# First expert's weights loaded and split during attention, with a guessed expert

## The chip, the cores and the metric

The kernel runs on one core of a Trainium2 chip. The metric is the device time of one execution in microseconds (us). Matmuls run on TensorE (PE; PEld is its weight load), elementwise work on VectorE (DVE), ScalarE (ACT) and GpSimd (POOL); SyncE (SP) issues most of the transfers.

## The reference

Three layers follow one another on 2304 tokens (4 batches of 576) of width 512:

```python
scores = scale * np.matmul(q, k.transpose(0, 1, 3, 2))      # 8 heads of 64
scores = np.where(masks[None], scores, -1e9)                 # 4 heads: window 32; 4 heads: window 128, every 4th
attn = softmax(scores);  x = (attn @ v), heads side by side  # (2304, 512)

logits = x @ w_gate + modality_bias[modality_id]             # 8 experts, 2 modalities
e_idx = argmax(logits);  gate_w = softmax(logits)[e_idx]
out[mask_e] = gate_w * (relu(x[mask_e] @ w1[e]) @ w2[e])     # 512 -> 1024 -> 512, one expert per token

h = relu(x @ w_in);  out = (h * h) @ w_out                   # 512 -> 2048 -> 512
```

`modality_bias` is drawn with a spread of 0.5, and it decides most of the routing. In the inputs used here both modalities have their largest bias at expert 1 (0.93 and 0.47). After two batches expert 1 has 989 tokens and expert 4 has 163; after all four they have 1982 and 322, and no other expert has any.

## The kernel before

**Precision.** Matrices of the two later layers are split into a high part (`Copy` on ACT into the reduced type) and a low part (source minus high part, on DVE); each product is three matmuls: high by high, high by low, low by high.

**Attention** works in 48 units of 96 queries by 4 heads. `schedule` runs one round per unit and writes the order of all engines out by hand. In round i, PE gets the mask and the scores of unit i (`A`, lines 335 and 338), the transposes of the attention output x of unit i-5 (`H`, L413), the transposes of the probabilities of unit i-2 (`D`, L360) and their product with v for unit i-3 (`F`, L374). DVE gets the row maximum `nm` of unit i (L341), the low part `xtl` of unit i-5 (L417), and for unit i-3 the sum, reciprocal and scaled output `rs`, `rc`, `x` (L377, L380, L383). ACT gets the high part `xth` (L416), the copy `pt` of the transposes (L362) and last the exponentials `p` of unit i (L350, four instructions). Before the experts start, `H` has one PSUM bank, so its transposes wait until `xtl` of the round before has read it. Every sixth round and the next have the logits' matmuls (L434). Six units share a load of q, k and v on SP; POOL scales q (L316). Each unit's x goes to DRAM (`xd`) by SP.

**Routing.** After every batch of 12 units, `batch` routes it in small steps between the attention's instructions: about 30 DVE instructions of 0.15 to 0.3 us, one-hots, a table of token numbers. From the second batch on, `select` names the slots that are full: an expert and 128 of its tokens. It writes for each slot the expert, whether it differs from the slot before (`esel`), and where the tokens stand.

**Experts.** A slot j is gathered from `xd` by an indirect DMA (`begin`), transposed and split (`tx`, L747 to L749), multiplied with w1 (`l1`, 24 matmuls of 512 columns, L761), transposed again (`th`) and multiplied with w2 (`l2`, 24 more, L791). There are 25 slots in the program; 19 are run here, and their weights change only where the expert does. Slots come in waves: 2 after the second batch, 4 after the third, the rest after the fourth. `filler` puts slot work into the attention's rounds, FILL units of cost (about 1 us each) per round.

**The first slot** is special: its expert is known only after the second batch is routed, so then SP loads w1 and w2 (2 MB each, L710), ACT and DVE split them; POOL takes the low part of the first two of the four pieces of w1 (L720), and the eight pieces of w2 are split between the steps of `l1`. Later slots load under a condition on SP (L708) and split under a branch (`split`, L727): they do both only when the expert changes.

**The last layer** (`Ffn`) starts when attention's memory is free; its w_in and w_out are decoded from 8-byte floats beside the slots and it takes the second half of the time (L1010, 384 columns, and L1064, 512 columns).

The functions that the change touches, with the line numbers of the profile:

Of the kernel before, what the change touches and what calls it, by code (L numbers as in the profile page):

```python
# [11 lines left out]
F32 = mybir.dt.float32  # L12
# [29 lines left out]
RATE, RATE1, RATE2, FILL, BURST, GAP = 0.35, 0.5, 0.5, 3.0, 0.0, 3  # L42
# [22 lines left out]
def body(ctx, tc, ins, out):  # L65
# [14 lines left out]
    g.nsl = const.tile([1, 1], I32, name="nsl")  # L80

# [31 lines left out]
def schedule(g, att, moe):  # L113
# [3 lines left out]
    early = None  # L117
    i = 0
# [37 lines left out]
    for i in itertools.count():  # L156
        att.tail = i >= nu + 2
        ns, no, nh = (2, (5,), (5,)) if att.tail else (2, (5,), (6,)) if moe.ready else (3, (5, 4), (7,))
        r = RATE2 if i >= nu + 5 else RATE1 if moe.prepped else RATE
        if i == nu + 6:  # L160
            att.units.close()
            early = Early(g)
        if i == nu + 2:
            moe.banks((2, 4), (6, 0), (1, 1), (7, 3))
        att.A(i, (0, 1, 2)[:ns])
        if i == SETUP:
            att.setup()
        if NTL < i <= nu + 5 and i % NTL == 5:
            att.logits(i // NTL - 1, 1)
            if moe.ready and not att.tail:  # L170
                no, nh = nh, no
        if i > hold:
            step(r)
        att.H(i - 5, nh)
        filler(FILL / 2, False)
        att.D(i - 2)
        step(r)
        att.F(i - 3, no, one)
        att.C(i)
        filler(FILL / 2, True)  # L180
        step(r)
        if NTL < i <= nu + 5 and i % NTL == 4:
            att.logits(i // NTL - 1, 0)
        if due and side is None:
            moe.ready = sum(WAVES[due - 1])
            moe.pump()
            due = 0
        if nxt < B and side is None and i >= (nxt + 1) * UPB + 5:
            side = att.batch(nxt)
            due, sc, hold = nxt, 0.0, i + 1  # L190
            nxt += 1
        if not more:
            break
# [7 lines left out]
class Attention:  # L201
    def __init__(self, g, ctx):
# [27 lines left out]
        self.pref = al.tile([QT, E], F32, name="pref")  # L230
        self.tok = al.tile([QT, TPB], F32, name="tok")
# [24 lines left out]
    def setup(self):  # L256
# [20 lines left out]
        nc.vector.tensor_tensor(out=self.bias, in0=self.bias, in1=btmp, op=ALU.add)  # L277

    def bank(self):
        return self.g.bk[5 if self.tail else 6]  # L280
# [292 lines left out]
    def select(self, j0, n):  # L573
# [36 lines left out]
        if j0 == 0:  # L610
            yield 0.12
            nc.vector.memset(ef[:, 0:1], -1.0)
# [59 lines left out]
class Moe:  # L672
    def __init__(self, g, ctx):
# [10 lines left out]
        self.gx = [wp.tile([128, XW], F32, name=f"gx{i}") for i in range(3)]  # L684
        self.xh = wp.tile([128, 4, 128], F32R, name="xh")
        self.xl = wp.tile([128, 4, 128], F32R, name="xl")
        self.y = [wp.tile([128, XW], F32, name=f"y{i}") for i in range(2)]
# [14 lines left out]
    def stage(self, j, w):  # L702
# [4 lines left out]
        if j:  # L707
            nc.sync.dma_start(out=self.st[w], in_=src, cond=c, cond_hint=False)  # L708
        else:
            nc.sync.dma_start(out=self.st[w], in_=src)  # L710

    def split(self, j, w):
# [5 lines left out]
        def part(k, eng=nc.vector):  # L718
            nc.scalar.activation(out=hi[:, k, :], in_=src[:, k, :], func=AF.Copy)
            eng.tensor_tensor(out=lo[:, k, :], in0=src[:, k, :], in1=hi[:, k, :].bitcast(F32), op=ALU.subtract)  # L720

        if j == 0:
            for k in range(n):
                part(k, nc.gpsimd if w == 0 and k < 2 else nc.vector)
                yield -1
            return
        with tc.If(c > 0, preferred_fallthrough_block=False):  # L727
            for k in range(n):
                part(k)
# [83 lines left out]
    def prep(self, j):  # L813
# [4 lines left out]
        yield from self.split(j, 0)  # L818
# [6 lines left out]
    def main(self, j):  # L825
# [3 lines left out]
        w2 = self.split(0, 1) if j == 0 else iter(())  # L829
        for c in self.l1(j):  # L830
            next(w2, None)
            yield c
# [7 lines left out]
        yield from self.split(j, 1) if j else w2  # L840
# [319 lines left out]
```

## Time and profile before

| | |
|---|---|
| median of 3 runs | 801.3 us (796.3, 801.3 and 968.0) |
| the profiled execution | 797.15 us, of which the span of the trace is 795.4 us |
| mean granted TensorE clock | 0.997 |
| PE busy | 773.7 us, 97% of the span |
| PE weight load | 668.5 us, 84% |
| DVE busy | 413.0 us, 52% |
| ACT busy | 325.2 us, 41% |
| POOL busy | 170.0 us, 21% |

The times that follow are from the profiled execution and count from the start of its span. PE is busy nearly throughout, so the shares say little; what counts is where PE is not busy, and how many microseconds that is. Attention alone runs from 6 to about 117 us, attention with the first slots to about 160 us, the other slots to about 390 us, and the last layer to the end.

### The profile page before, as it was taken

How to read it: one execution, taken by the hardware profiler on the slowest of the kernel's cores; microseconds unless marked ns; L12 is line 12 of the kernel's file. 1: busy time of each engine (PE TensorE's matmuls, PEld its weight loads, DVE VectorE, ACT ScalarE, POOL GpSimd, SP SyncE). 2: the span in 40 equal slices, each digit the busy share in tenths (PEclk: the TensorE clock that was granted, in tenths of full speed). 3: DMA queues.
4: the chain of work that ended last, by engine and by line, in shares of the span. 5: the costliest groups of instructions: out<-in, count | busy, mean ns of one | idle time of the engine just before them, and what ended most of it. 6: DMA issues, size and time to landing. Idle time of an engine off the chain costs nothing.

```text
span 795.4 us, 12643 instructions
## 1 busy us (share of the span) xinstructions
PE 773.7 (97%) x4273; PEld 668.5 (84%) x4273; DVE 413.0 (52%) x1136; ACT 325.2 (41%) x779; POOL 170.0 (21%) x222
## 2 busy tenths in 40 slices
PE   8999997999999999999999999999999999999996
PEld 5888875778888888887888999999998998999985
DVE  5787889568456777452389822332242233234232
ACT  5877767334345545552245422222232232232221
POOL 4145632226323333201034400010010001001001
PEclk9999999999999999999999999999999999999999
DMA  8666773235534444451445210010010001001001
GB/s 228 178 165 176 179 250 100 74 93 148 172 111 128 134 112 129 146 185 55 147 147 160 67 40 27 14 41 27 1 54 0 27 14 40 1 0 40 1 1 40
DMA packets 49130, 72.65 MB, mean 91 GB/s; under 512 B 7296, under 2 KB 31712, under 8 KB 48544
## 3 DMA queue, kind: packets, MB, share of 16 engines
q1 hardware_dynamic: 43040, 56.00, 24.3%
q0 software_dynamic: 3280, 10.76, 4.4%
q10 hardware_dynamic: 2736, 4.99, 1.7%
q8 instruction: 35, 0.57, 0.3%
q14 instruction: 39, 0.32, 0.1%
HBM read 132.27 MB, written 17.06 MB: 188 GB/s over the span
## 4 chain that ended last, share of the span: by engine, by line
issue 40%; PE 9%; POOL 2%; POOLq 0%; DVE 0%
PE bk L1010 4%; PE bk L1064 4%; POOL out L1069 2%; PE bk L791 1%; PE bk L993 0%; POOLq L1156 0%; DVE fout L1068 0%; POOLq L1069 0%
## 5 line engine op out<-in xcount | busy, mean ns | idle before, releaser
L1020 DVE TENSOR_TENSOR fsq<-fr 128x384 f32<-128x384 f32 x96 | 53.4, 557 | 163.6 <-ACT fr L1018 163.5
L1010 PE MATMUL bk<-yh,wih 128*128 128x384 f32 x384 | 130.0, 338 | 2.1 <-ACTq L860 1.4
L1010 PE MATMUL bk<-yh,wil 128*128 128x384 f32 x384 | 129.2, 336 | 0.0
L1010 PE MATMUL bk<-yl,wih 128*128 128x384 f32 x384 | 129.0, 336 | 0.0
L1018 ACT ACTIVATE fr<-bk 128x384 f32<-128x384 f32 x96 | 47.0, 490 | 193.0 <-PE bk L1010 192.4
L1064 PE MATMUL bk<-woh,fhh 128*128 128x512 f32 x288 | 113.2, 393 | 0.0
L1064 PE MATMUL bk<-woh,fhl 128*128 128x512 f32 x288 | 112.7, 391 | 0.0
L1064 PE MATMUL bk<-wol,fhh 128*128 128x512 f32 x288 | 112.6, 391 | 0.0
L1069 POOL DMA_INDIRECT out<-fout,fidx x18 | 17.6, 978 | 322.1 <-DVE fout L1068 321.8
L1029 DVE TENSOR_TENSOR fhl<-fsq,fhh 128x384 fp32r<-128x384 f32 x96 | 55.3, 576 | 44.3 <-ACT fhh L1028 44.1
L1010 PEld LDWEIGHTS bk<-yh,wih 128*128 128x128 f32 x384 | 72.2, 188 | 4.7 <-ACTq L860 1.7
L1010 PEld LDWEIGHTS bk<-yl,wih 128*128 128x128 f32 x384 | 72.2, 188 | 1.8
L1010 PEld LDWEIGHTS bk<-yh,wil 128*128 128x128 f32 x384 | 72.2, 188 | 0.0
L1028 ACT ACTIVATE fhh<-fsq 128x384 fp32r<-128x384 f32 x96 | 50.4, 525 | 51.1 <-DVE fsq L1020 50.9
L1064 PEld LDWEIGHTS bk<-woh,fhl 128*128 128x128 f32 x288 | 54.0, 188 | 12.3
L761 PE MATMUL bk<-w1h,xh 128*128 128x512 f32 x152 | 63.1, 415 | 0.8 <-DVE htl L777 0.8
L1064 PEld LDWEIGHTS bk<-wol,fhh 128*128 128x128 f32 x288 | 54.1, 188 | 9.6
L1064 PEld LDWEIGHTS bk<-woh,fhh 128*128 128x128 f32 x288 | 54.1, 188 | 9.5
L791 PE MATMUL bk<-w2h,hth 128*128 128x512 f32 x152 | 61.1, 402 | 0.0
L761 PE MATMUL bk<-w1h,xl 128*128 128x512 f32 x152 | 61.0, 401 | 0.0
L761 PE MATMUL bk<-w1l,xh 128*128 128x512 f32 x152 | 60.8, 400 | 0.0
L791 PE MATMUL bk<-w2h,htl 128*128 128x512 f32 x152 | 59.5, 391 | 0.0
(174 smaller groups left out, 1356.3 us busy)
## 6 DMA issues: line engine op xcount, KB each, us to landing
st<-in_w SPq DMA_DIRECT2D x41, 2048.0 KB
raw<-in_wi SPq DMA_DIRECT2D x32, 256.0 KB
raw<-in_wo SPq DMA_DIRECT2D x32, 256.0 KB
v<-in_v SPq DMA_DIRECT2D x7, 780.0 KB
q<-in_q SPq DMA_DIRECT2D x7, 576.0 KB
kd<-in_k SPq DMA_DIRECT2D x14, 288.0 KB
xd<-x SPq DMA_DIRECT2D x40, 96.0 KB
yb<-y ACTq DMA_DIRECT2D x13, 256.5 KB
```

The lines of the kernel that those rows point to most:

```text
L761: nc.tensor.matmul(ps, a[:, c, :], w[:, c, sl], start=k == 0, stop=k == 11)
L791: nc.tensor.matmul(ps, a[:, c, :], w[:, c, :], start=k == 0, stop=k == 23)
L1010: nc.tensor.matmul(ps, w[:, c, f * 128:(f + 1) * 128], a[:, c, :], start=k == 0, stop=k == 11)
L1018: nc.scalar.activation(out=r, in_=ps, func=AF.Relu)
L1020: nc.vector.tensor_tensor(out=s, in0=r, in1=r, op=ALU.mult)
L1028: nc.scalar.activation(out=hh, in_=s, func=AF.Copy)
L1029: nc.vector.tensor_tensor(out=hl, in0=s, in1=hh.bitcast(F32), op=ALU.subtract)
L1064: nc.tensor.matmul(acc[t], a[:, sl], w[:, f, :], start=f == 0 and j == 0, stop=f == NF - 1 and j == 2)
L1069: dma = nc.gpsimd.indirect_dma_start(out=out, out_offset=bass.IndirectOffsetOnAxis(ap=self.idx[:, i:i + 1].bitcast(U32), axis=0), in_=o, i ...
```

## The change

A guess of the first slot's expert is computed in `setup` from the modality bias alone: for each modality the experts with the largest bias are marked, and the guess is the marked expert of the lowest number (eight small DVE instructions, stored in a new 4-byte tile `guess`). A new generator `Moe.first` loads that expert's w1 and w2 in 16 pieces of 256 KB on SP and splits each piece two calls later, the high part on ACT and the low part on DVE. `schedule` calls it at the end of rounds: three rounds of four up to round 17, then even rounds in which no routing is under way or routing holds. What is left is run before the first wave is made ready. `select` starts with the guess in place of -1, so that the first slot loads and splits only if the guess was wrong, under the same condition and branch as later slots. In the first wave `filler` gets 2.0 units per round (FILL1) in place of 3.0. The routing's matmuls use bank 7 in place of 6 once slots are ready. `xh` and `xl`, the split inputs of `l1`, are allocated ahead of the gather buffers `gx`.

```diff
-RATE, RATE1, RATE2, FILL, BURST, GAP = 0.35, 0.5, 0.5, 3.0, 0.0, 3
+RATE, RATE1, RATE2, FILL, FILL1, BURST, GAP = 0.35, 0.5, 0.5, 3.0, 2.0, 0.0, 3
...
     g.nsl = const.tile([1, 1], I32, name="nsl")
+    g.guess = const.tile([1, 1], I32, name="guess")
...
+    first = moe.first()
...
-        filler(FILL / 2, False)
+        f = (FILL1 if moe.ready == WAVES[0][1] else FILL) / 2
+        filler(f, False)
...
-        filler(FILL / 2, True)
+        filler(f, True)
...
+        if i > SETUP and (i % 4 < 3 if i < UPB + 6 else i % 2 == 0 and (side is None or i < hold)):
+            next(first, None)
         if due and side is None:
+            run(first)
             moe.ready = sum(WAVES[due - 1])
...
+        self.first = al.tile([1, 16], F32, name="gfirst")[:, :1]
...
+        top = ac.tile([1, 2, 1], F32, name="gtop")
+        at = ac.tile([1, 2, E], F32, name="gat")
+        cum = ac.tile([1, E], F32, name="gcum")
+        nc.vector.tensor_reduce(out=top, in_=mb[0:1], axis=AX.X, op=ALU.max)
+        nc.vector.tensor_tensor(out=at, in0=mb[0:1], in1=top.to_broadcast([1, 2, E]), op=ALU.is_equal)
+        nc.vector.tensor_tensor(out=at[:, 0], in0=at[:, 0], in1=at[:, 1], op=ALU.max)
+        nc.vector.tensor_tensor_scan(out=cum, data0=at[:, 0], data1=at[:, 0], initial=0.0, op0=ALU.add, op1=ALU.bypass)
+        nc.vector.tensor_scalar(out=at[:, 1], in0=cum, scalar1=0.5, scalar2=None, op0=ALU.is_lt)
+        nc.vector.tensor_reduce(out=self.first, in_=at[:, 1], axis=AX.X, op=ALU.add)
+        nc.vector.tensor_scalar(out=self.first, in0=self.first, scalar1=float(E - 1), scalar2=None, op0=ALU.min)
+        nc.vector.tensor_copy(g.guess, self.first)
 
     def bank(self):
-        return self.g.bk[5 if self.tail else 6]
+        return self.g.bk[5 if self.tail else 7 if self.g.moe.ready else 6]
...
-            nc.vector.memset(ef[:, 0:1], -1.0)
+            nc.vector.tensor_copy(ef[:, 0:1], self.first)
...
-        self.gx = [wp.tile([128, XW], F32, name=f"gx{i}") for i in range(3)]
         self.xh = wp.tile([128, 4, 128], F32R, name="xh")
         self.xl = wp.tile([128, 4, 128], F32R, name="xl")
+        self.gx = [wp.tile([128, XW], F32, name=f"gx{i}") for i in range(3)]
...
-        if j:
-            nc.sync.dma_start(out=self.st[w], in_=src, cond=c, cond_hint=False)
-        else:
-            nc.sync.dma_start(out=self.st[w], in_=src)
+        nc.sync.dma_start(out=self.st[w], in_=src, cond=c, cond_hint=False)
+
+    def first(self):
+        nc, ins = self.g.nc, self.g.ins
+        e = nc.values_load(self.g.guess[0:1, 0:1], engines=(ET.SP,), min_val=0, max_val=E - 1)
+        parts = []
+        for w in range(2):
+            st, hi, lo = (x[w].rearrange("p c f -> p (c f)") for x in (self.st, self.wh, self.wl))
+            src = ins["w1" if w == 0 else "w2"][bass.ds(e, 1)].rearrange("o p c f -> p (o c) f")
+            for k in range(8):
+                parts.append([x[:, k * 512:(k + 1) * 512] for x in (st, src, hi, lo)])
+        for i in range(len(parts) + 2):
+            if i < len(parts):
+                nc.sync.dma_start(out=parts[i][0], in_=parts[i][1])
+            if i > 1:
+                st, _, hi, lo = parts[i - 2]
+                nc.scalar.activation(out=hi, in_=st, func=AF.Copy)
+                nc.vector.tensor_tensor(out=lo, in0=st, in1=hi.bitcast(F32), op=ALU.subtract)
+            yield
...
-        def part(k, eng=nc.vector):
-            nc.scalar.activation(out=hi[:, k, :], in_=src[:, k, :], func=AF.Copy)
-            eng.tensor_tensor(out=lo[:, k, :], in0=src[:, k, :], in1=hi[:, k, :].bitcast(F32), op=ALU.subtract)
-
-        if j == 0:
-            for k in range(n):
-                part(k, nc.gpsimd if w == 0 and k < 2 else nc.vector)
-                yield -1
-            return
         with tc.If(c > 0, preferred_fallthrough_block=False):
             for k in range(n):
-                part(k)
+                nc.scalar.activation(out=hi[:, k, :], in_=src[:, k, :], func=AF.Copy)
+                nc.vector.tensor_tensor(out=lo[:, k, :], in0=src[:, k, :], in1=hi[:, k, :].bitcast(F32), op=ALU.subtract)
...
-        yield from self.split(j, 0)
+        self.split(j, 0)
...
-        w2 = self.split(0, 1) if j == 0 else iter(())
-        for c in self.l1(j):
-            next(w2, None)
-            yield c
+        yield from self.l1(j)
...
-        yield from self.split(j, 1) if j else w2
+        self.split(j, 1)
```

In the built program the 16 splits stand at the end of rounds 6; 8, 9, 10; 12, 13, 14; 16, 17, 18; 22; 24; 26; 28; 30 and 34. Line numbers shift by 7 to 25; L742 is the new low part, L741 the new high part, L738 the new load.

The first place is DVE in rounds 7 to 9 of the attention (x closes a round, nm opens the next; xtl is the low part for the logits). Before:

```order
L383 TENSOR_TENSOR x<-bk_72,rc 96x256
L341 TENSOR_REDUCE nm<-bk_68 96x4
L417 TENSOR_TENSOR xtl<-bk_75,xth 128x2x96
L377 TENSOR_SCALAR rs<-bk_73 96x4
L380 RECIPROCAL rc<-rs 96x4
L383 TENSOR_TENSOR x<-bk_73,rc 96x256
L341 TENSOR_REDUCE nm<-bk_69 96x4
```

and with the change:

```order
L401 TENSOR_TENSOR x<-bk_72,rc 96x256
L742 TENSOR_TENSOR w1l<-st_84,w1h 128x512
L359 TENSOR_REDUCE nm<-bk_68 96x4
L435 TENSOR_TENSOR xtl<-bk_75,xth 128x2x96
L395 TENSOR_SCALAR rs<-bk_73 96x4
L398 RECIPROCAL rc<-rs 96x4
L401 TENSOR_TENSOR x<-bk_73,rc 96x256
L742 TENSOR_TENSOR w1l<-st_84,w1h 128x512
L359 TENSOR_REDUCE nm<-bk_69 96x4
```

The low part stands between x and the next round's nm, so nm waits for it.

The second place is ACT in the same rounds, with the change (before, the rows are the same without L741):

```order
L368 ACTIVATE p<-bk_70,nm 96x128 x4
L741 ACTIVATE w1h<-st_84 128x512
L434 ACTIVATE xth<-bk_75 128x2x96
L380 ACTIVATE pt<-bk_71 128x384
L368 ACTIVATE p<-bk_68,nm 96x128 x4
L741 ACTIVATE w1h<-st_84 128x512
L434 ACTIVATE xth<-bk_75 128x2x96
```

The high part stands behind the exponentials of its round and ahead of the next round's xth; the low part on DVE needs it.

The third place is PE where the first slot begins (gx are its gathered tokens, w1h, w1l and xh, xl the operands of `l1`). Before, two attention rounds lie between the slot's transposes (gx) and its first matmuls; these are the last rows of the second:

```order
L374 MATMUL bk_73<-v,pt 96x65 x4
L335 LDWEIGHTS mask
L335 MATMUL bk_69<-mask 96x512
L338 MATMUL bk_69<-kd_145,q 96x256 x2
L413 MATMUL bk_74<-ident,x 128x96 x2
L360 MATMUL bk_71<-ident,p 128x96 x4
L374 MATMUL bk_73<-v,pt 96x65 x4
L761 MATMUL bk_70<-w1h,xh 128x512
L761 MATMUL bk_70<-w1l,xh 128x512
L761 MATMUL bk_70<-w1h,xl 128x512
```

With the change:

```order
L772 MATMUL bk_70<-ident,gx_95 128x128 x4
L378 MATMUL bk_71<-ident,p 128x96 x4
L392 MATMUL bk_73<-v,pt 96x65 x4
L751 UNCONDITIONAL_BRANCH
L786 MATMUL bk_70<-w1h,xh 128x512
L786 MATMUL bk_70<-w1l,xh 128x512
L786 MATMUL bk_70<-w1h,xl 128x512
```

The first matmuls follow the transposes in the same round, two rounds earlier.

## Rows read from the trace of the kernel before

**Rows 1.** Stages: length, busy time of each engine (instructions), PE clock, DMA share, GB/s.
```profile
20.00:100.00 80.00, 80.00 (x684) 68.08 (x682) 62.89 (x219) 61.22 (x203) 36.90 (x54) 1.00 0.69 175
100.00:120.00 20.00, 18.11 (x147) 14.58 (x147) 17.07 (x81) 12.93 (x43) 6.51 (x10) 1.00 0.76 257
120.00:140.00 20.00, 14.92 (x87) 11.29 (x85) 18.57 (x46) 14.49 (x34) 4.67 (x2) 0.91 0.30 87
140.00:160.00 20.00, 17.84 (x113) 14.03 (x112) 10.70 (x52) 5.96 (x13) 4.66 (x8) 1.00 0.27 71
400.00:780.00 380.00, 380.00 (x1950) 345.04 (x1949) 154.15 (x309) 113.00 (x240) 39.48 (x37) 1.00 0.11 35
```

**Rows 2.** PE's waits, 100 to 160 us: releaser, total us, times, longest.
```profile
PE bk L374 <- DVE x L383: 4.3, 3, 3.0
...
PE bk L434 <- DVE xtl L417: 0.8, 1, 0.8
...
PE bk L477 <- DVE xtl L417: 0.5, 1, 0.5
PE bk L434 <- DVE lt L438: 0.5, 1, 0.5
PE bk L451 <- DVE xtl L417: 0.5, 1, 0.5
```

**Rows 3.** Timeline at the first slot's split: start, duration, engine, instruction [idle before].
```profile
121.01 4.67 POOL L720 TENSOR_TENSOR w1l<-st,w1h 128x1024 fp32r<-128x1024 f32 x2 [10.36 <-ACT w1h L719]
...
121.50 1.89 DVE L526 CAST rrf<-rri 96x6 f32<-96x6 int32 x1
...
127.46 0.89 PE L374 MATMUL bk<-v,pt 128*96 128x65 f32 x8 [3.05 <-DVE x L383]
```

**Rows 4.** Timeline, the first slot's first matmuls on PE, first and last of seven.
```profile
128.85 0.63 PE L761 MATMUL bk<-w1h,xl 128*128 128x512 f32 x1
...
131.41 0.63 PE L761 MATMUL bk<-w1h,xl 128*128 128x512 f32 x1
```

**Rows 5.** Timeline of one plain attention round, 35.04 to 37.28 us, main rows.
```profile
35.03 1.12 ACT L350 ACTIVATE p<-bk,nm 96x128 f32<-96x128 f32 x4
35.04 0.38 PE L335 MATMUL bk<-mask 96*96 96x512 bf16 x1
...
35.64 0.42 DVE L383 TENSOR_TENSOR x<-bk,rc 96x256 f32<-96x256 f32 x1
...
36.12 0.33 PE L413 MATMUL bk<-ident,x 96*128 96x96 f32 x2
...
36.33 0.69 DVE L341 TENSOR_REDUCE nm<-bk 96x4 f32<-96x512 f32 x1 [0.26 <-PE bk L338]
...
36.93 0.34 DVE L417 TENSOR_TENSOR xtl<-bk,xth 128x192 fp32r<-128x192 f32 x1
...
37.28 0.38 PE L335 MATMUL bk<-mask 96*96 96x512 bf16 x1
```

**Rows 6.** Instructions on tile st: count, duration ns min/median/max, first and last start.
```profile
L719 ACT ACTIVATE w2h<-st x16: 622/629/642, 130.7 to 355.8; 128x512 fp32r<-128x512 f32 x16
L720 DVE TENSOR_TENSOR w2l<-st,w2h x16: 668/675/692, 132.6 to 357.4; 128x512 fp32r<-128x512 f32 x16
```

**Rows 7.** PE's waits, 0 to 20 us, the longest.
```profile
PE bk L338 <- DMA kd<-in_k: 2.2, 2, 1.1
```

**Rows 8.** By line: a DVE and a POOL instruction, duration ns min/median/max.
```profile
L506 DVE TENSOR_TENSOR rpo<-rcum,rtot x4: 196/196/351, 54.9 to 171.6; 96x48 f32<-96x48 f32 x4
...
L316 POOL TENSOR_SCALAR q<-q x45: 680/687/721, 9.5 to 103.5; 128x192 f32<-128x192 f32 x45
```

**Rows 9.** By line: 512-column matmuls, duration ns min/median/max.
```profile
L761 PE MATMUL bk<-w1l,xh x152: 391/397/628, 128.5 to 368.7; 128*128 128x512 f32 x152
...
L791 PE MATMUL bk<-w2l,hth x152: 387/389/397, 153.8 to 387.8; 128*128 128x512 f32 x152
...
L1064 PE MATMUL bk<-wol,fhh x288: 387/389/475, 396.9 to 788.4; 128*128 128x512 f32 x144
```

More of the change, by code (lines that the diff above doesn't have):

```diff
@@ L706, in stage @@
         src = src[bass.ds(e, 1)].rearrange("o p c f -> p (o c) f")
-        if j:
-            nc.sync.dma_start(out=self.st[w], in_=src, cond=c, cond_hint=False)
-        else:
-            nc.sync.dma_start(out=self.st[w], in_=src)
+        nc.sync.dma_start(out=self.st[w], in_=src, cond=c, cond_hint=False)
[5 more added lines that the diff above has]
+            st, hi, lo = (x[w].rearrange("p c f -> p (c f)") for x in (self.st, self.wh, self.wl))
+            src = ins["w1" if w == 0 else "w2"][bass.ds(e, 1)].rearrange("o p c f -> p (o c f)")
+            for k in range(8):
[8 more added lines that the diff above has]
+            yield
     def split(self, j, w):
```

## The prediction

> **What bounds the kernel now.** I read the stages first, then PE's waits, then the timeline where PE waits. PE is busy for all of 20 to 100 us and of 400 to 780 us, so most of the time is PE's own work, and the change takes none of it away [rows 1]. What can be won is where PE stands idle or runs slowly. Between 100 and 160 us, where attention meets the first slots, PE is busy 18.11 + 14.92 + 17.84 = 50.87 of 60 us: 9.1 us are lost. In 120 to 140 us the granted clock is 0.91, a further 0.09 x 20 = 1.8 us [rows 1]. The reader should see three things there. PE's longest waits are for x, an attention result that DVE delivers late: 4.3 us in three waits, one of 3.05 us [rows 2, 3]. DVE is late because it stands in the first slot's split: while POOL takes two low parts of w1 (4.67 us), a cast of 6 numbers takes DVE 1.89 us [rows 3]. After the 3.05 us PE runs at its lower level, 1.2 GHz: seven matmuls start 2.56 / 6 = 0.43 us apart and last 0.63 us, where the same form has a median of 0.397 us [rows 4, 9].
>
> **The change, part by part.** The sum is made against the profiled execution, 797.15 us; that is 0.85 us over the lowest of the three runs and 4.15 us under their median.
>
> *Removed: load and split of the first slot between 110 and 140 us.* The guess is expert 1, and the first slot's expert is the lowest one with 128 tokens after two batches, also expert 1, so load and split are skipped there. Of the 9.1 us, 2.3 us stay: the waits of the logits and of routing for xtl and lt (0.8 + 0.5 + 0.5 + 0.5), which come before the slots or have nothing to do with the split [rows 2]. The waits for x and those that follow from DVE's backlog go: 9.1 - 2.3 = 6.8 us. The slow clock goes with the 3.05 us wait ahead of it: 1.8 us. What is late next: the slot's matmuls now follow its transposes in the same round, and need xh and xl from ACT and DVE in between. The trace has no such place; between nothing and the 2.2 us that 140 to 160 us lost [rows 1] I take 0.7, nearer to nothing because the loads and pieces that crowd DVE there are gone.
>
> *Added: 16 splits in the attention's rounds.* A plain round takes PE 2.24 us without a gap, mask to mask [rows 5]. The high part (0.63 us) stands behind the exponentials p, the low part (0.68 us) on DVE needs it, and nm of the next round stands behind the low part [rows 6]. For a split by itself: p ends 1.11 us into the round, the low part at 1.11 + 0.63 + 0.68 = 2.42, and nm, which started at 36.33 - 35.04 = 1.29, is 1.13 us late, and xtl with it. PE needs that xtl for its transposes in the next round: they start at 38.36, xtl ended at 37.27, so 1.09 us are to spare [rows 5]. A lone split costs PE some 0.05 us. A split in the next round too finds no slack left: the ring nm, p, high part, low part, nm takes 0.69 + 1.12 + 0.63 + 0.68 = 3.12 us in place of 2.24, 0.88 us more. Six of the 16 follow on a split in the round before (rounds 9, 10, 13, 14, 17, 18): 6 x 0.88 + 10 x 0.05 = 5.8 us. Rounds with logits are longer on PE and rounds with routing longer on DVE; I let the two cancel. Bounds: 16 x 0.05 = 0.8 us if there is more slack than I see, 16 x 0.88 = 14.1 us if none.
>
> The low part reads two SBUF operands while POOL runs 36.9 of 80 us [rows 1]. The nearest row is L506, which also reads two: 351 ns at most against 196, 0.155 us more, and the nearest case of that is the start of a POOL op [rows 8]. 16 x 0.46 x 0.155 = 1.1 us. Bounds: 0, and 16 x 0.69 = 11.0 us if each low part waits out a whole q scaling.
>
> *Added: 16 loads of 256 KB on SP.* Eleven pieces in rounds 4 to 17 (about 35 us) are 82 GB/s on top of 175, 257 together; 100 to 120 us carried 257 GB/s at a share of 0.76 [rows 1]. Each piece has two calls, over 4 us, to land. Cost 0. Queued behind them on SP are the loads of q, k and v and the writes of x. If that cover goes, it shows as PE waiting for keys, as twice at the start (2.2 us in two waits) [rows 7]; for five later groups up to 5.5 us.
>
> *Added: eight small DVE instructions for the guess.* About 8 x 0.2 = 1.6 us by L506 [rows 8], in rounds in which PE waits 1.1 us for keys anyway [rows 7]; 0.2 us, bounds 0 and 1.6.
>
> *FILL1 and bank 7.* They move slot work between rounds; where PE is the limit this costs nothing. Bank 7 is where l2 adds up, but in the built order the first l2 comes after routing of the third batch has left it; 0, at most 0.5 as the wait for lt [rows 2].
>
> *Moved: xh and xl.* L761, whose stationary operand is xh or xl, has a median of 397 ns; L791 and L1064, of the same 512 columns, 389 [rows 9]. xh and xl start 32 bytes past a multiple of 64, those of L791 and L1064 at a multiple. The new tile guess moves everything behind it by 32 bytes, so now all of them stand 32 past. If the address made the 8 ns and the move cures it: 456 x 0.008 = -3.6 us. If 32 past is the cause: 456 + 864 matmuls x 7 or 8 ns = +9.6 us. The 384-column matmuls, also with operands 32 past, run without a gap in 400 to 780 us, which tells neither; I take 0 and keep both ends.
>
> The sum: 797.15 - 6.8 - 1.8 + 0.7 + 5.8 + 1.1 + 0.2 = **796.4 us**.
>
> **The rivals.**
>
> *A, splits hidden.* If ACT and DVE run far enough ahead, all 16 cost as lone ones: 796.4 - 5.0 = 791.4, with the address gain 787.8. For: DVE and ACT are busy only 62.9 and 61.2 of 80 us [rows 1]. Against: that is an average, and the ring crosses both engines in series [rows 5]. 0.22.
>
> *B, slower: the addresses.* All 512-column matmuls go at L761's pace, 796.4 + 9.6 = 806.0. It decides from 0.6 ns per matmul on, (797.15 - 796.4) / 1320. For: the difference follows the operand [rows 9]. Against: other things differ too, banks among them. 0.12. The Trainium skill, TensorE: Matmul & The Clock Gate, Step-by-step: what each phase is for, says that weight loads have a read port of their own and take nothing from a running matmul's operand. By that rule B has no chance; the 397 against 389 keeps it one.
>
> *C, slower: the low parts held up by POOL.* Each waits out a q scaling: 796.4 - 1.1 + 11.0 = 806.3, slower than before from 0.8 us of extra wait in all. For: 1.89 us for a cast under POOL's low part [rows 3]. Against: L506 lost 0.155 us, not the rest of a 0.69 us scaling [rows 8]. 0.09. The Trainium skill, SBUF — State Buffer, SBUF: two separate sides, has a rule for this: the port pair of DVE and GpSimd is an exclusive lock, and a DVE op with two SBUF inputs and a GpSimd op that reads SBUF block each other for the whole instruction. The trace agrees for the cast and not in full for L506.
>
> *D, the guess misses.* Then load and split return to the gap beside the 16: 796.4 + 6.8 + 1.8 - 0.7 = 804.3. Only with other inputs; 0.01.
>
> *E, the loads are late*, 5.5 us more: 801.9. 0.04.
>
> **How the numbers follow.** The forecast, splits paid by what the gap gives back, has 0.52, and by itself 793 to 801. The likeliest single time is 796.4. The range reaches down into A and up to B and C: 788 to 806. Two per cent, about what a measurement of this kernel can tell from no change, is 16 us. All that can be won is 9.1 + 1.8 + 3.6 = 14.5 us, so faster by more has 0.01; slower by more needs B and C at once, or the full bound of the splits with one of them: 0.03. Within: 0.96.
>
> **What would show it.** Right: no weight load near 110 us; PE idle in 100 to 160 us down to about 3 us, with a clock of 1.00 throughout; and new waits of L431's transposes for xtl between 25 and 60 us, some 0.9 us in rounds 10, 11, 14, 15, 18 and 19, about 6 us in all. No such waits means A. L816 and the last layer's 512-column matmuls at 397 ns means B. Low parts of over 1 us beside POOL means C. A load of 2 MB after 110 us means D. Waits for kd or q mean E. I am wrong if PE's idle time after 100 us stays near 9 us.

## The result, and the profile after

The changed kernel takes **807.4 us** (median of 4 runs, 805.97 to 811.13), the kernel before 800.9 beside it: a ratio of 1.0117, 95% interval 1.009 to 1.0145, so 9.4 us slower by the ratio. The ratio goes by the fast executions alone, and the two medians are only 6.5 us apart. The forecast was 796.4 us, with a range of 788 to 806. The profiled execution is the slowest of the four, 811.13 us with a span of 809.4, 14.0 over the span before.

The stages of the changed kernel, columns as in [rows 1]:

```profile
20.00:40.00 20.00, 15.21 (x117) 12.31 (x116) 12.16 (x35) 13.21 (x44) 3.96 (x6) 0.90 0.77 213
40.00:60.00 20.00, 17.10 (x113) 12.84 (x113) 12.23 (x34) 11.96 (x39) 3.96 (x6) 0.85 0.70 182
60.00:80.00 20.00, 18.03 (x150) 14.58 (x149) 16.52 (x63) 14.12 (x46) 9.49 (x14) 1.00 0.60 164
80.00:100.00 20.00, 20.00 (x175) 16.97 (x174) 16.56 (x52) 16.08 (x52) 7.21 (x11) 1.00 0.77 216
100.00:120.00 20.00, 18.78 (x157) 15.28 (x156) 17.15 (x66) 14.98 (x50) 14.46 (x20) 1.00 0.63 161
120.00:140.00 20.00, 17.39 (x133) 13.70 (x131) 16.41 (x79) 11.73 (x38) 5.18 (x9) 0.96 0.41 106
140.00:160.00 20.00, 18.81 (x129) 15.40 (x128) 12.30 (x49) 9.53 (x28) 0.00 (x0) 0.96 0.06 16
160.00:180.00 20.00, 16.31 (x94) 12.58 (x93) 7.59 (x36) 4.94 (x10) 4.62 (x8) 1.00 0.29 86
```

Two things are to be seen. Attention, where PE had no gap from 20 to 100 us [rows 1], now loses 4.8 + 2.9 + 2.0 = 9.7 us, and its granted clock falls to 0.90 and 0.85. And the gap after attention is still there: 1.2 + 2.6 + 1.2 + 3.7 = 8.7 us from 100 to 180 us. PE's waits, first from 20 to 100 us, then from 100 to 180 (of both the longest), say what it waits for:

```profile
PE bk L431 <- DVE xtl L435: 5.0, 6, 2.2
PE bk L452 <- ACT lt L458: 3.9, 1, 3.9
...
PE bk L452 <- DVE lt L456: 2.0, 1, 2.0
PE bk L772 <- DMA gx<-xd,sc: 1.5, 1, 1.5
PE bk L786 <- ACTq L751: 1.1, 1, 1.1
...
PE bk L431 <- DVEq L751: 0.8, 1, 0.8
PE bk L786 <- DVEq L751: 0.5, 1, 0.5
```

None of the waits of the product with v for x in [rows 2] is left. In their place stand waits for the conditional blocks of skipped splits (L751; the 0.8 us is for a later slot's block), for the third slot's gathered rows (gx) and for the last logits (lt). The longest wait of all, 3.9 us, lies in attention. The timeline there:

```profile
22.97 0.37 SPq L328 DMA_DIRECT2D q<-in_q  x1
23.40 1.21 SPq L336 DMA_DIRECT2D kd<-in_k  x2
...
25.44 0.49 SPq L738 DMA_DIRECT2D st<-in_w  x1
26.48 1.92 SPq L405 DMA_DIRECT2D xd<-x  x2
...
31.90 0.29 PE L452 MATMUL bk<-xtl,wg 128*16 128x288 f32 x1
...
33.91 0.63 ACT L741 ACTIVATE w1h<-st 128x512 fp32r<-128x512 f32 x1 [2.45 <-DMA st<-in_w]
...
36.97 0.38 ACT L458 ACTIVATE lt<-bk 16x288 f32<-16x288 f32 x1
...
37.41 0.42 PE L452 MATMUL bk<-xth,wg 128*16 128x288 f32 x1 [3.87 <-ACT lt L458]
37.62 0.44 PE L452 MATMUL bk<-xtl,wg 128*16 128x288 f32 x1
```

The high part at 33.91 is the third split, and its piece was asked for at 25.44: it needed 8.5 us, where the forecast gave it "over 4". ACT stands idle for 2.45 us with xth, pt, p and lt queued behind it. PE needs lt to empty the one logits bank and waits 3.87 us, and after that its clock is at the lower level: the same 288 columns take 0.44 us in place of 0.29. ACT has three such waits for st in 20 to 100 us, 4.8 us in all.

How many us each stretch of rounds lost against the kernel before, worked out from the starts of the mask matmuls that open the 48 rounds (the run with one piece and the run with four calls are told of below):

| rounds, counted from 1 | what stands in them | changed | one piece | four calls | low part late |
|---|---|---|---|---|---|
| 1 to 7 | start | 0.9 | 0.4 | 0.9 | 2.6 |
| 8 to 12 | 8 to 10 plain, 11 and 12 logits | 6.8 | 2.7 | 0.7 | 0.0 |
| 13 to 16 | plain | 2.0 | 0.8 | 0.9 | 0.0 |
| 17 to 19 | logits | 4.2 | 1.1 | 1.2 | 0.0 |
| 20 to 23 | routing | 2.6 | 2.2 | 2.3 | 0.5 |
| 24 to 32 | plain, logits | 0.1 | 0.1 | 0.1 | 1.1 |
| 33 to 40 | routing | 1.7 | 1.8 | 1.6 | 0.6 |
| 8 to 40 | all with splits | 17.3 | 8.7 | 6.7 | 2.2 |

And the matmuls, by line with min/median/max in ns, that answer to [rows 9]:

```profile
L786 PE MATMUL bk<-w1l,xh x152: 387/389/628, 137.9 to 382.7; 128*128 128x512 f32 x152
...
L816 PE MATMUL bk<-w2h,hth x152: 389/389/478, 167.7 to 401.8; 128*128 128x512 f32 x152
```

L786 is the L761 of before: 389 ns in place of 397; L816, the L791 of before, is what it was, and so are the last layer's 512-column matmuls (L1086, a median of 389). Over the 648 matmuls of the slots from the 97th to the 745th the changed kernel needs 166.1 us, that of before 168.1.

### The profile page after: what moved, and what is told of

It reads as the page before. It is cut to its first block, busy times and chain, and to the rows that moved or that the text cites. A ratio compares the mean times of both kernels' runs of the same rounds, so it can differ in the third digit from the quotient of the medians.

```text
span 809.4 us, 12733 instructions
## 1 busy us (share of the span) xinstructions
PE 778.2 (96%) x4273; PEld 672.1 (83%) x4273; DVE 412.4 (51%) x1150; ACT 323.3 (40%) x783; POOL 165.1 (20%) x220
## 4 chain that ended last, share of the span: by engine, by line
issue 40%; DVE 4%; POOL 2%; DMA 2%; PE 1%; ACT 1%; SPq 0%; POOLq 0%; ACTq 0%; DVEq 0%
POOL out L1091 2%; DMA raw<-in_wo 2%; DVE fhl L1051 1%; DVE da L914 1%; PE bk L816 1%; DMA yb<-y 1%; DVE da L920 1%; DVE da L909 1%; DVE fsq L1042 0%; POOL wol L925 0%; ACT fhh L1050 0%; PE bk L1032 0%; SPq L1072 0%; ACT dm L907 0%; DVE da L917 0%
## 5 line engine op out<-in xcount | busy, mean ns | idle before, releaser
L1086 PE MATMUL bk<-woh,fhh 128*128 128x512 f32 x288 | 112.6, 391 | 0.0
L1086 PE MATMUL bk<-wol,fhh 128*128 128x512 f32 x288 | 112.5, 391 | 0.0
L1086 PE MATMUL bk<-woh,fhl 128*128 128x512 f32 x288 | 112.3, 390 | 0.0
L1086 PEld LDWEIGHTS bk<-woh,fhl 128*128 128x128 f32 x288 | 54.1, 188 | 11.7
L786 PE MATMUL bk<-w1h,xh 128*128 128x512 f32 x152 | 62.2, 409 | 1.5 <-ACTq L751 1.1
L1086 PEld LDWEIGHTS bk<-wol,fhh 128*128 128x128 f32 x288 | 54.1, 188 | 9.4
L1086 PEld LDWEIGHTS bk<-woh,fhh 128*128 128x128 f32 x288 | 54.1, 188 | 9.4
L368 ACT ACTIVATE p<-bk,nm 96x128 f32<-96x128 f32 x192 | 53.9, 363 | 19.6 <-DVE nm L359 14.8
L816 PE MATMUL bk<-w2h,hth 128*128 128x512 f32 x152 | 61.2, 402 | 0.0
L786 PE MATMUL bk<-w1l,xh 128*128 128x512 f32 x152 | 59.6, 392 | 0.5 <-DVEq L751 0.5
L786 PE MATMUL bk<-w1h,xl 128*128 128x512 f32 x152 | 59.8, 393 | 0.0
```

The source lines that it names most:

```text
L368: self.g.nc.scalar.activation(out=p[:, h, :], in_=ps[:, h, :], func=AF.Exp, bias=nm[:, h:h + 1], scale=1.0)
L786: nc.tensor.matmul(ps, a[:, c, :], w[:, c, sl], start=k == 0, stop=k == 11)
L816: nc.tensor.matmul(ps, a[:, c, :], w[:, c, :], start=k == 0, stop=k == 23)
L1086: nc.tensor.matmul(acc[t], a[:, sl], w[:, f, :], start=f == 0 and j == 0, stop=f == NF - 1 and j == 2)
```

## The experiments

All ratios are against the kernel before on the same chip; a thousandth is 0.8 us. A difference of two rows carries the intervals of both, which makes about 3 us either way.

| run | ratio | 95% interval | us against before |
|---|---|---|---|
| changed kernel | 1.0117 | 1.009 to 1.0145 | +9.4 |
| e1_move: only xh and xl moved | 0.997 | 0.9947 to 0.9994 | -2.4 |
| e3_none: no loads, no splits | 0.991 | 0.9878 to 0.9943 | -7.2 |
| e4_loads | 0.9924 | 0.9894 to 0.9954 | -6.1 |
| e5_splits: one piece | 1.0031 | 1.0015 to 1.0047 | +2.5 |
| e6_lead: four calls | 1.0006 | 0.9989 to 1.0024 | +0.5 |
| e7_fill3 | 1.010 | 1.007 to 1.013 | +8.0 |
| e8_noif | 1.0046 | 1.0025 to 1.0067 | +3.7 |
| e9_lead_low: and low part late | 0.9928 | 0.9901 to 0.9956 | -5.8 |
| e10_if_first: and blocks first | 0.995 | 0.9935 to 0.9965 | -4.0 |
| e11_move_dve | 0.9964 | 0.9945 to 0.9984 | -2.9 |
| e12_none_first | 0.9907 | 0.9879 to 0.9935 | -7.4 |
| e13_none_noif | 0.9888 | 0.9862 to 0.9915 | -9.0 |
| e14_lead_low, again | 0.9934 | 0.9909 to 0.9959 | -5.3 |
| e15_if_first, again | 0.9941 | 0.9919 to 0.9964 | -4.7 |

### Where xh and xl stand

e1_move: the kernel before with

```
-        self.gx = [wp.tile([128, XW], F32, name=f"gx{i}") for i in range(3)]
         ...
         self.xh = wp.tile([128, 4, 128], F32R, name="xh")
         self.xl = wp.tile([128, 4, 128], F32R, name="xl")
+        self.gx = [wp.tile([128, XW], F32, name=f"gx{i}") for i in range(3)]
```

> The kernel before with the one edit that xh and xl stand ahead of gx in SBUF; no guess, no early split. Theory 'place': the 6 ns by which the 456 first-layer matmuls follow each other faster in the changed kernel (0.2275 us apart in place of 0.2335) come from this move alone: 456 x 0.006 = 2.7 us, so 0.3 to 0.4 per cent below the kernel before, and a median of 389 ns in place of 397. Rival 'pad': they come from the 32 bytes that the tile guess puts ahead of the weights; then 397 ns and the time of before.

e2_pad: the kernel before with `g.guess = const.tile([1, 1], I32)` behind `g.nsl`, as in the changed kernel: ahead of the weights and all that follows them. It was timed once, at 796.99 us.

> The kernel before with a tile of 32 bytes put ahead of everything else in SBUF and nothing moved: the weights, hth and htl then stand 32 bytes past a multiple of 64, xh and xl at a multiple, the reverse of before. Theory 'place': what made xh and xl slow is where they stand, not the remainder: the first layer's matmuls keep 397 ns and the others 389. Rival 'same remainder': slow is a pair whose two operands differ in the remainder: 397 for the first layer too (w1 32, xh 0), 389 for the second (both 32). Rival 'remainder of the stationary operand': 389 for the first layer and 397 for the second.

e1_move has medians of 389 and 390 ns, and gains 2.4 us: 'place' holds. e2_pad, where every remainder by 64 bytes is the reverse of before, by line:

```profile
L762 PE MATMUL bk<-w1l,xh x152: 392/397/628, 128.3 to 368.7; 128*128 128x512 f32 x152
...
L792 PE MATMUL bk<-w2h,hth x152: 389/389/481, 153.2 to 387.4; 128*128 128x512 f32 x152
```

The first layer keeps its 397 ns, the second its 389. Rival B of the prediction, whichever way its remainder is read, is gone. What it is about the place 6 KB further on stays open.

### Loads and splits, each alone

e3_none takes loads and splits out, e4_loads the splits; in both POOL clears the weights. e5_splits keeps the splits, all of one piece:

```
 for i in range(len(parts) + 2):
-    if i < len(parts):
-        nc.sync.dma_start(out=parts[i][0], in_=parts[i][1])        # e3, e5 (e5: if i == 0)
     if i > 1:
-        nc.scalar.activation(out=hi, ...); nc.vector.tensor_tensor(out=lo, ...)
+        nc.gpsimd.memset(hi, 0.0); nc.gpsimd.memset(lo, 0.0)        # e3, e4
```

> The changed kernel with neither the 16 loads nor the 16 splits; POOL clears the first slot's weights with 32 memsets in their place, so the first expert's rows are not computed. What is left of the change is what it does after the attention's rounds, and the place of xh and xl. Forecast's theory (the gap gives back 6.8 + 1.8 - 0.7 = 7.9 us): with 2.7 us of the move, 10.6 below before, near 790. Rival (new waits stand in the gap, which gives back the 2.2 us that the rounds after 120 us show): 2.2 + 2.7 = 4.9 below before, near 796.

> The changed kernel with the 16 loads but without the 16 splits (32 POOL memsets clear the weights in their place; the first expert's rows are not computed). If the loads cost the attention anything by themselves, through q, k and v that come later, this stands above the kernel without both: theory 'contention' 3 to 5 us above it. If a load costs only because ACT stands waiting for it: equal to the kernel without both, within 1 us.

> The changed kernel with all 16 splits, each of the same piece, so one load of 256 KB in place of 16 (the first expert's rows are wrong in this run). Theory 'ring' (the forecast's: ACT's high part and DVE's low part lengthen the round whatever the loads do): all of the 15.6 us that the rounds from 21 to 86 us lost are still there, the time equals the changed kernel's, about 807. Theory 'landing' (ACT stands in order behind a piece that has not landed, and PE runs at its lower clock after the wait): the rounds with an ACT wait for st and their slow followers go, 5.5 + 1.1 + 2.9 + 1.3 = 10.8 us less, about 797.

The four form a square: neither -7.2, loads +1.1 on that, splits +9.7, both +16.6. So 16.6 - 1.1 - 9.7 = 5.8 us, with some 4 us either way by the four intervals, come only when both are there, as 'landing' says; by the traces of rounds 8 to 40 it is 4.6 us. 'Landing' foretold 797 for e5, and 801.8 came, so 'ring' has more than half.

e4_loads lost 1.1 us by the times and 4.0 by its trace, all in rounds 24 to 32, against e3_none with the same memsets. PE never waits for q, k or v itself, but POOL, which scales q, waits longer for it. First POOL in e3_none, then POOL and PE in e4_loads:

```profile
55.02 4.03 POOL L334 TENSOR_SCALAR q<-q 128x192 f32<-128x192 f32 x6 [5.86 <-DMA q<-in_q]
...
58.17 3.96 POOL L334 TENSOR_SCALAR q<-q 128x192 f32<-128x192 f32 x6 [6.80 <-DMA q<-in_q]
...
70.20 0.22 PE L568 MATMUL bk<-rval,rhot 96*128 96x144 f16 x1 [0.87 <-POOL rval L556]
```

With the loads q is ready for POOL 3.15 us later, and the routing's rval behind it starts 3.08 us later, for which PE waits 0.87 and 1.19 us. The memsets, about 0.5 us each on POOL ahead of rval, add to this wait; the changed kernel, which has none, does not show it.

e3_none has little to fear in attention: its 41st round starts at 102.50 us, that of before at 102.48. So its -7.2 are the move's 2.4 and 4.8 of the gap, where the forecast took 7.9. By the trace it is less: from the start of the 41st round to the 97th matmul of the slots 63.69 us in place of 66.28, 2.6, and 63.90, 2.4, in the changed kernel; 72 of those matmuls at 6 ns, 0.4, belong to the move. But the same stretch took e1_move, which has the old split there, 68.51 us, 4.8 above e3_none, and e2_pad 66.20. So what the gap gave back lies between 2.4 and 4.8 us, and no run says it closer.

### Earlier loads, later low parts

e6_lead asks for a piece four calls ahead; e9_lead_low also issues the low part one call later:

```
-    for i in range(len(parts) + 2):
+    for i in range(len(parts) + 4):          # e9: + 5
-        if i > 1:  ... parts[i - 2]: high, low
+        if i > 3:  ... parts[i - 4]: high, low
# e9:
+        if i > 4:  ... parts[i - 5]: low
+        if 3 < i < len(parts) + 4:  ... parts[i - 4]: high
```

> The changed kernel with four calls in place of two between a piece's load and its split; nothing else, except that the splits begin two calls later (rounds 9, 10, 12 to 14, 16 to 18, 22, 24 and so on to 38). Theory 'landing': pieces have landed when ACT comes to them, PE's waits for lt (3.9 us) and after ACT's 1.5 us wait go, and the time falls by the 5.7 us by which loads and splits together exceed the two alone, to the 801 to 802 us of the kernel with one piece. Rival 'bandwidth': the pieces are late however early they are asked for, or q, k and v become late in their place: no change, 806 to 808.

> As the run with four calls between load and split, and each low part is issued one call after its high part, so that on DVE it no longer waits for ACT's high part of the same round, and nm behind it does not either. Theory 'ring' (a split costs because nm, p, high part, low part and nm stand in series over both engines, 3.12 us a round): the cost of the splits, 9.7 us with one piece, falls to what ACT's own work per round exceeds PE's round, (1.12 + 0.63 + 0.33 + 0.49) - 2.24 = 0.33 in place of 0.88 us in dense rounds, so to about 4 us: 796 to 797. Rival 'work' (DVE and ACT simply have too much to do in rounds with logits and routing): no faster than the run with four calls, 801 to 802.

e6_lead fell by 1.0117 - 1.0006, **8.9 us**: more than the 5.7 foretold, since its splits also begin two calls later, with fewer of them in the dense rounds. By the table above that part is about 2 us (8.7 with one piece, 6.7 with four calls, the difference in rounds 8 to 12). ACT no longer waits for a piece, while the DMA moves more, 239 GB/s from 20 to 60 us where the changed kernel moved 198: 'bandwidth' is gone, the lead was too short. The end of three splits in plain rounds (at the ends of rounds 13 to 15), timeline of e6_lead:

```profile
41.94 0.68 DVE L359 TENSOR_REDUCE nm<-bk 96x4 f32<-96x512 f32 x1
...
42.72 1.13 ACT L368 ACTIVATE p<-bk,nm 96x128 f32<-96x128 f32 x4 [0.82 <-DVE nm L359]
...
42.94 0.39 PE L431 MATMUL bk<-ident,x 96*128 96x96 f32 x2 [0.61 <-DVE xtl L435]
...
43.73 0.63 ACT L741 ACTIVATE w1h<-st 128x512 fp32r<-128x512 f32 x1
...
44.40 0.79 DVE L742 TENSOR_TENSOR w1l<-st,w1h 128x512 fp32r<-128x512 f32 x1 [0.78 <-ACT w1h L741]
...
45.10 0.68 DVE L359 TENSOR_REDUCE nm<-bk 96x4 f32<-96x512 f32 x1
...
46.10 0.38 PE L431 MATMUL bk<-ident,x 96*128 96x96 f32 x2 [0.70 <-DVE xtl L435]
```

From nm to nm 3.16 us: the forecast's ring, 3.12. DVE stands 0.78 us idle for the high part with nm queued behind. PE waits 0.61 us for xtl in round 16 and 0.70 in round 17. And the same place of e9_lead_low:

```profile
41.40 0.68 DVE L359 TENSOR_REDUCE nm<-bk 96x4 f32<-96x512 f32 x1
...
43.04 0.68 DVE L741 TENSOR_TENSOR w1l<-st,w1h 128x512 fp32r<-128x512 f32 x1
...
43.19 0.63 ACT L744 ACTIVATE w1h<-st 128x512 fp32r<-128x512 f32 x1
...
43.64 0.68 DVE L359 TENSOR_REDUCE nm<-bk 96x4 f32<-96x512 f32 x1
```

The low part is that of the piece before, waits for nothing, and nm to nm is 2.24 us, PE's own pace. The 16 splits and loads cost 2.2 us in rounds 8 to 40 (1.5 in the trace of e14_lead_low, the same kernel); half of it stands in rounds 24 to 32, where PE waits 0.94 us for rval of POOL. The run is at 0.9928, 0.9934 on another chip: **5 to 6 us faster than the kernel before**, the lowest ratios of those that compute the whole, with intervals that overlap those of e10 and e15.

### The gap

e7_fill3 sets FILL1 to 3.0. e8_noif returns from split for the first slot ahead of its conditional block. e10_if_first is e9_lead_low with the two blocks ahead of the slot's transposes:

```
     def prep(self, j):
+        if j == 0:
+            self.split(0, 0); self.split(0, 1)
         self.tx(j)
         ...
-        self.split(j, 0)
+        if j: self.split(j, 0)          # and in main: if j: self.split(j, 1)
```

e12_none_first and e13_none_noif make the edits of e10 and e8 in e3_none.

> The changed kernel with FILL1 at 3.0, so that a round of the first wave takes as much slot work as before the change. The forecast's view (slot work moves between rounds at no cost): equal to the changed kernel, within 0.5 us of 807. Rival (the first two slots' work is all there is to cover the waits of the last rounds, and more of it per round is used up sooner): slower, by up to 3 us, with more PE waits for lt and gx before the third slot. Third: the wait behind the last rounds is shorter when the first slots are done sooner, up to 2 us faster.

> The changed kernel without the first slot's two conditional splits, which here are skipped anyway since the guess is right (with another guess this kernel would compute with the wrong expert). If PE's waits of 1.13 and 0.54 us ahead of the first slot's matmuls are for the places of these conditional blocks in ACT's and DVE's queues (behind the exponentials p and behind x), they and the slow clock after them go: 1.7 + 1.6 = 3.3 us, to 804. If they are for xh and xl themselves, the waits stay under other names: within 0.7 us of the changed kernel, 807.

> The run with late low parts and four calls' lead, and the first slot's two conditional splits issued ahead of its transposes in place of behind them, so that ACT and DVE come to them before the last exponentials and x of that round; nothing is left out, with another guess the splits are done there. Theory 'queue place': PE's waits of 1.1 and 0.5 us ahead of the first slot go, with the slow clock behind them and the 0.8 us wait behind the second block: the 3.7 us that the run without these blocks gained between the 41st round and the third slot. So 0.9928 - 3.7 / 800 = 0.988 of the kernel before, 790 to 791. Rival 'block': a conditional block costs ACT and DVE the time wherever it stands: 0.993, 796.

> The changed kernel with neither loads nor splits in the attention (POOL clears the first slot's weights, the first expert's rows are not computed), and the first slot's two conditional blocks issued ahead of its transposes. The same kernel with the blocks in their old place had 0.991 of before. Theory 'queue place': 2.4 us less, what the trace of the full kernel gained between the 41st round and the third slot: 0.988. Rival 'block': 0.991.

> As the run without loads and splits, and without the first slot's two conditional blocks at all. Theory: the blocks cost 3.7 us between the 41st round and the third slot, so 0.991 - 0.0046 = 0.9865. If a block's cost comes back later as a wait for logits or gathers: 0.990 to 0.991.

> The run with four calls' lead and late low parts once more, on one chip with the three others. 0.9928 of before, as measured; 3.0 to 3.5 us above the run without loads and splits with its blocks in the same place, which is then all that sixteen splits and loads cost.

> The run with four calls' lead, late low parts and the conditional blocks first, on the same chip as the one with the blocks behind the transposes. Theory 'queue place': 2.4 us or 0.003 below it, 0.990. Rival 'block': the two are equal; the two measured so far, on two chips, gave 0.995 and 0.9928.

FILL1 makes no difference that can be told: 1.010 and 1.0117 with overlapping intervals. Its trace shows that the waits change places: PE waits 1.78 us for xtl before the last logits and not for gx.

The block costs something. In the changed kernel PE's first slot, timeline:

```profile
135.64 1.12 ACT L368 ACTIVATE p<-bk,nm 96x128 f32<-96x128 f32 x4
...
136.86 0.50 PE L786 MATMUL bk<-w1h,xh 128*128 128x512 f32 x1 [1.13 <-ACTq L751]
...
137.37 0.42 DVE L401 TENSOR_TENSOR x<-bk,rc 96x256 f32<-96x256 f32 x1
137.90 0.50 PE L786 MATMUL bk<-w1l,xh 128*128 128x512 f32 x1 [0.54 <-DVEq L751]
...
139.41 0.63 PE L786 MATMUL bk<-w1h,xl 128*128 128x512 f32 x1
```

The first matmul starts 0.10 us after p ends on ACT at 136.76, the second 0.11 after x ends on DVE: the skipped block has nothing to do, but stands behind them. Then the clock is down, 0.63 us for a matmul. Without the blocks (e13_none_noif, PE's waits from 100 to 165 us):

```profile
PE bk L452 <- DVE lt L456: 2.0, 1, 2.0
PE bk L772 <- DMA gx<-xd,sc: 1.6, 1, 1.6
...
PE bk L431 <- DVEq L751: 0.8, 1, 0.8
PE bk L786 <- DVE row L775: 0.6, 1, 0.6
```

0.6 us are left, for the operands themselves (xl on DVE, just ahead of row): what the forecast took 0.7 for. e8_noif is 5.7 us below the changed kernel, but its trace has shorter waits for lt in attention too (3.2 in place of 3.9); in its gap, measured as above, 60.18 in place of 63.90, 3.7 us. In the kernel without loads and splits it is 63.69 to 60.79 by the trace, 2.9. By the times of one chip it is 0.9907 to 0.9888, 1.5 us, from e12_none_first, whose blocks stand ahead of the transposes, to e13_none_noif, with intervals that overlap.

Their place is another matter. The traces gain with the blocks first (64.31 to 61.91 us from e9 to e10, 65.83 to 61.78 from e14 to e15), the times don't: 0.9934 against 0.9941 on one chip, 0.9907 for e12 where e3 had 0.991. The profiled executions of e9 and e14 are the slowest of their kernels, so the traces favour e10 and e15. With the blocks first PE waits 1.44 us for xl. 'Queue place' is not borne out as a cure; how much of the block's cost is its place stays open.

### POOL's part of the old split

e11_move_dve is e1_move with `part(k)` in place of `part(k, nc.gpsimd if w == 0 and k < 2 else nc.vector)`.

> The kernel before with xh and xl moved, and the two low parts of w1 that POOL took given to DVE. The prediction read DVE's 1.89 us for a cast of six numbers beside POOL's 4.67 us low part as the cause of PE's 3.05 us wait for x. If POOL's low parts cost DVE by holding it up: 1 to 3 us faster than the same kernel with POOL's part (0.997 of before), so 0.993 to 0.996. If DVE's queue is simply too long there, two more low parts of 1.3 us on it make it 2 to 3 us slower: 1.000.

The times are equal, 0.9964 and 0.997, which neither side foretold. DVE in e1_move, with POOL's part, and then in e11_move_dve:

```profile
121.82 1.79 DVE L526 CAST rrf<-rri 96x6 f32<-96x6 int32 x1
...
123.79 2.19 DVE L537 TENSOR_SCALAR rhot<-iota,rrf 96x128 f16<-96x128 f32 x1
...
121.48 0.16 DVE L526 CAST rrf<-rri 96x6 f32<-96x6 int32 x1
...
122.95 0.28 DVE L537 TENSOR_SCALAR rhot<-iota,rrf 96x128 f16<-96x128 f32 x1
```

So POOL's low parts did hold DVE up: the cast and the rhot behind it take 0.44 us without them and 3.98 with them. But the two low parts take DVE 1.23 and 1.21 us when it does them itself. The longest wait for x falls from 3.04 to 2.27 us, and DVE's queue stays long. The prediction read [rows 3] rightly; the one delay is exchanged for the other.

## Why the prediction was wrong, step by step

**The loads, "cost 0": the step that failed.** "Each piece has two calls, over 4 us, to land": the third took 8.5 us. Ahead of it on SP, since the piece before, stood the loads of q and keys and a write of x; two more writes came behind it. The forecast looked for lateness at PE, as waits for kd or q (rival E, 5.5 us), but the one who waits is ACT, in order, with attention's own work behind it. That costs 16.6 - 9.7 = 6.9 us against e5_splits, which has the same splits in the same rounds, the slow clock behind the waits included; e6_lead gains 8.9, of which about 2 are its later splits.

**The gap, 6.8 + 1.8 - 0.7 = 7.9 us: not given back in full.** The waits for x went as forecast, but the gap gave back 2.4 us by the trace of the changed kernel and 4.8 by the times of e3_none less e1_move. "What is late next" was asked for xh and xl, 0.7 us, and measured at 0.6 without the blocks. Missed were the skipped block on both engines, 1.5 to 3.7 us with the slow clock after it, and new waits for the last logits (2.0 us, 0.5 before [rows 2]) and the third slot's gather (1.5). That these come because the first two slots' work is done sooner and no longer covers them is argued and not shown: e7_fill3, which does it sooner still, only moves the waits. The mark set for being wrong, idle time after 100 us near 9 us, was met: 8.7.

**The splits, 5.8 + 1.1 = 6.9: somewhat too small.** In the forecast's rounds and with the piece there (e5_splits) they cost 9.7 us by the times and 8.7 by the trace in rounds 8 to 40; two calls later (e6_lead) 7.7 and 6.7. The ring is there, 3.16 us, and in plain rounds its price is the forecast's: the three splits behind rounds 13 to 15 of e6_lead cost 0.83 us in round 16 and 1.17 in round 17, where two times 0.88 were taken, and four lone ones cost 0.1 together in rounds 24 to 32. "I let the two cancel", of rounds with logits and routing, was wrong where routing stands on DVE: rounds 20 to 23, behind three splits, cost 2.3 us where two times 0.88 were taken, and rounds 33 to 35, behind a lone one, 1.6 where 0.05 was.

**The low parts beside POOL, 1.1: nothing; rival C fell.** They take 0.69 us, one in 16 0.89. It is POOL that waits. In e5_splits:

```profile
27.92 4.67 POOL L334 TENSOR_SCALAR q<-q 128x192 f32<-128x192 f32 x6 [8.58 <-DMA q<-in_q]
28.29 0.69 DVE L742 TENSOR_TENSOR w1l<-st,w1h 128x512 fp32r<-128x512 f32 x1 [0.92 <-ACT w1h L741]
31.35 0.69 DVE L742 TENSOR_TENSOR w1l<-st,w1h 128x512 fp32r<-128x512 f32 x1 [0.78 <-ACT w1h L741]
...
31.46 1.13 POOL L334 TENSOR_SCALAR q<-q 128x192 f32<-128x192 f32 x1
...
93.12 3.96 POOL L334 TENSOR_SCALAR q<-q 128x192 f32<-128x192 f32 x6 [11.32 <-PE bk L392]
```

Six scalings take 3.96 us alone and 4.67 with two low parts beside them: the two scalings that start under a low part take 0.95 and 1.13 us (the second at 31.46) in place of 0.69. The low part at 28.29 keeps its 0.69 us, though it starts 0.37 us into a scaling. The Trainium skill, SBUF — State Buffer, SBUF: two separate sides, says that whichever of the two starts first has the port pair for its whole instruction; the trace agrees for a scaling that starts under a low part, and not for a low part that starts under a scaling.

**xh and xl, 0 with bounds of -3.6 and +9.6: a gain of 2.4.** 456 matmuls come 6 ns closer, 2.7 us; the times show 2.4. The Trainium skill's rule of a read port of their own for weight loads (TensorE: Matmul & The Clock Gate, Step-by-step: what each phase is for) gives no reason for a gain; the 397 against 389 ns are not explained by it.

**Right:** the guess holds, PE's new waits for xtl are there (5.0 us in six up to 100 us where about 6 were foretold, though the longest, 2.2, is behind a late piece), nothing like 4 MB moves from 130 to 160 us (16 GB/s from 140 to 160 us), FILL1 costs nothing that can be measured (bank 7 was not tried by itself), and the guess's eight instructions are not to be seen among PE's waits.

From -0.75 us (796.4 against 797.15): +6.9 for the loads, +2.8 for the splits (9.7 less 6.9), +3.1 for the gap (7.9 less 4.8), -2.4 for the move: +9.65. Measured were +9.4. The terms are differences along one chain of runs, so that they add up is no check of them, and each is known to about 3 us.

## What to carry to other kernels

Before work is laid into the slack of another stage, ask of each piece what stands behind it on its engine and when its data lands: a prefetch that is late costs nothing until an engine that runs in order comes to it, and then it costs everything behind it. Issue a dependent pair on two engines a step apart, so that neither waits for the other in the same round; here that turned 6.7 us of cost in rounds 8 to 40 into 2.2, and 1.5 in a second trace. A gap is a balance: work taken out of it uncovers the next wait, so price what it was covering.

## What was not expected of the hardware

- The same matmuls, 389 or 397 ns by where in SBUF their stationary operand stands, with the remainder by 64 bytes excluded as the cause (397 at 134880 and 134912 bytes of the partition, 389 at 128640 and 128672, worked out from the sizes of the tiles ahead). The cause is open.
- A conditional block that is skipped still holds up the engine that needs its result, until the block's own engine has come to it in its queue: PE started 0.10 and 0.11 us after ACT and DVE had ended the instruction ahead of it.
- PE ran on at its lower clock after some waits and not after others: after the 3.87 us wait the granted clock was 0.74 from 32 to 45 us, and the round that followed, without a wait, took 3.34 us in place of 2.23; after the 2.0 us wait for the last logits the same matmuls took 0.32 us as ahead of it, and the granted clock was 1.00 from 160 to 180 us.
